# A short convolution, a truncated Fourier mix and a product with its ReLU: x fetched two rows to a partition, the convolution worked by row parities in four quadrants of the array

## The chip, the cores and the metric

One core of one Trainium2 chip runs the whole kernel. The metric is the time of one execution in device microseconds (us); less is better. The kernel before was timed three times: median 177.82 us (177.51 to 178.9). A separate execution was profiled; its own time was 176.57 us.

## The reference

`x` has 8 sequences of 3264 rows and 192 columns (float32). `weight` has 7 taps for each of 8 heads; a head is 24 neighbouring columns. Three steps follow each other:

```python
# 1. causal convolution along the rows, one softmaxed 7-tap filter per head
w = softmax(weight, axis=-1)
c[b, s, h, :] = sum(w[h, k] * x_padded[b, s + k, h, :] for k in range(7))   # 6 zero rows in front
# 2. the 64 lowest Fourier modes of c along the rows, each multiplied by its own 192 x 192 complex matrix
C = rfft(c, axis=1)[:, :64]
Y = C @ (w_r + 1j * w_i)              # one matrix for each mode; the other modes are zero
u = c + irfft(Y, n=3264)
# 3. a product, a ReLU and a sum
out = u + maximum(u @ w_ch, 0)
```

The 64 complex matrices are 18.9 MB, `x` is 20.05 MB and `out` is 20.05 MB. The kernel fetches x and the matrices with a conversion to bfloat16 on the way.

## The kernel before

**Order.** The instructions of each engine stand in the order in which the program was written; the schedule is by hand, and the engines wait for each other by semaphores. All fetches of x and of the matrices are issued by POOL, in order; SP issues the stores. There are three stages.

**The convolution stage** works on four pairs of sequences (`q` is 0 to 3, two sequences `i` to each). A pair's rows are cut into 128-row tiles, one row to a partition, and `load_unit` (L141) fetches some tiles at a time: 13 double tiles (`b`) for each pair, in four units for the first pair and three for the others (`units`). A row of a tile is 192 values, so one DMA packet writes 384 bytes. The convolution along the rows is a matrix product with a banded matrix (`band`): row r of the output is a weighted sum of rows r-6 to r. The band is built at the start: seven masks (L178), seven predicated copies (L193) into `packed`, and four copies (L199, L201) that shift it for groups of 32 partitions. `conv_pass` (L269) does two heads of a unit: a main product with the tile itself and a corner product with the tile before it. Two instructions run side by side, each with 64 columns of the array (`tile_position` (0, 0) and (0, 64)); between them they give the even rows (`a` = 0) and the odd rows (`a` = 1) of a double tile as separate output tiles, which is the order that the later stages want. Results lie in three accumulators of two PSUM banks each (`ZC`), and ScalarE (L290) and VectorE (L292) take turns to copy them back over x in SBUF.

**The Fourier products** (`dft`, L295) are put between the passes: one output tile of c against a table of cosines and sines (`ftab`), 26 tiles to a pair, each as two instructions of 64 columns side by side. The table itself is computed by `table` (L206) on VectorE and ScalarE in three parts during the first pair; the dictionary `extra` says after which pass. When a pair is done, `xtrans` (L307) turns its result round.

**The mix stage** begins when all four pairs are done. `mix(g, bank)` (L421) multiplies with the matrices of four modes; g runs from 0 to 15. `load_w(g)` (L261) fetches the matrices in two DMAs; eight groups have places at once, and group 8 and later ones are fetched when an earlier `mix` has given its place free. Between the mixes `some` runs the transposes of c (L387) that the last stage needs.

**The output stage** (L642 and around it) forms u @ w_ch and the inverse transform in one accumulator for each tile, 64 rows of the array at a time; ScalarE applies the ReLU (L558), VectorE adds c (L545) and SP stores. There `turn` (L483) already exists: an empty instruction on TensorE that waits until named matmuls have ended, so that the lower and the upper half of the array do not write one PSUM bank at the same time.

## The time and the profile before

| what | value |
|---|---|
| median of three runs | 177.82 us (177.51 to 178.9) |
| the profiled execution's own time | 176.57 us |
| its span, first to last instruction | 174.6 us |
| TensorE matmul busy | 160.1 us (92%), 2756 instructions |
| VectorE, ScalarE, POOL busy | 122.0, 106.9, 58.6 us |
| granted TensorE clock | 0.995 of full speed |
| moved by DMA | 40.11 MB |
| convolution matmuls (L283) | 832 instructions, 39.1 us busy |
| Fourier products (L301) | 208 instructions, 20.9 us busy |
| copies back by VectorE (L292), by ScalarE (L290) | 26 for 24.8 us, 26 for 20.6 us |

Times in the profile count from the first instruction; the profiled execution took 1.97 us more than the span. A row of the list of groups gives the source line, the engine, the operation, what it writes and reads with its shape, how often it ran, then the busy time in us and the mean of one in ns, and after the bar the idle time of the engine just before. PE is TensorE's matmul, PEld its loading of the stationary operand, DVE VectorE, ACT ScalarE. The end of a matmul is modelled: the mean of one contains its way through the array, so the pace is read from starts, not from durations.

### The profile page before, as it was taken

What the parts mean: (1) busy time and instruction counts of PE and PEld (TensorE: products, weight loads), DVE (VectorE), ACT (ScalarE), POOL (GpSimd) and SP (SyncE); (2) the same over time, 40 slices, a digit from 0 to 9 for tenths busy, and PEclk for the clock granted to TensorE, in tenths of its full rate; (3) what the DMA queues carried; (4) which work ended last, traced back from release to release, by engine and by line L of the source; (5) the groups of instructions that cost most, each with busy time, mean ns of one, the idle gap of its engine ahead of it and who ended that gap; (6) DMA issues with size and microseconds to landing.
All of it is one profiled execution on the core that took longest, in us unless ns stands there. A gap on an engine that the chain in (4) does not pass through costs nothing.

```text
span 174.6 us, 6593 instructions
## 1 busy us (share of the span) xinstructions
PE 160.1 (92%) x2756; PEld 139.7 (80%) x2756; DVE 122.0 (70%) x226; ACT 106.9 (61%) x191; POOL 58.6 (34%) x101
## 2 busy tenths in 40 slices
PE   7967999999999988999967978999999999999990
PEld 2447989999998966899966545599999999999960
DVE  5669883274454562777745225699999999999991
ACT  6337885434544342787645244588788888887870
POOL 7999943465322344424344000592000000000000
PEclk9999999999999999999999999999999999999998
DMA  4999999999999999999999980289989899999896
GB/s 46 168 188 192 191 194 192 191 192 193 193 193 194 203 206 207 205 207 206 206 207 206 207 147 9 70 301 327 367 305 341 334 332 360 341 343 333 324 345 226
DMA packets 50541, 40.11 MB, mean 230 GB/s; under 512 B 28720, under 2 KB 50512, under 8 KB 50512
## 3 DMA queue, kind: packets, MB, share of 16 engines
q0 software_dynamic: 36000, 19.62, 81.2%
q1 hardware_dynamic: 14512, 20.09, 31.5%
q8 instruction: 21, 0.34, 0.8%
q14 instruction: 8, 0.07, 0.1%
HBM read 39.10 MB, written 20.05 MB: 339 GB/s over the span
## 4 chain that ended last, share of the span: by engine, by line
PE 72%; DMA 13%; DVE 5%; ACT 4%; issue 2%; POOL 1%; DVEq 0%; POOLq 0%; ACTq 0%
PE z L642 33%; PE z L283 19%; DMA arena<-in_moe_w_i_dram 13%; PE z L301 10%; PE z L387 4%; DVE arena L193 2%; PE z L426 2%; ACT xall L290 1%; DVE xall L292 1%; PE z L569 1%; POOL xall L148 1%; PE z L512 1%; ACT L184 1%; DVE arena L545 1%; PE z L316 1%
## 5 line engine op out<-in xcount | busy, mean ns | idle before, releaser
L545 DVE TENSOR_TENSOR arena<-z,xall 128x384 f32<-128x384 f32 (+1 forms) x104 | 57.5, 557 | 3.1 <-PE z L642 1.1
L558 ACT ACTIVATE z<-z 128x384 f32<-128x384 f32 x102 | 48.3, 475 | 12.6 <-PE z L642 3.6
L642 PE MATMUL z<-arena,ftab 64*128 64x384 bf16 x308 | 45.3, 323 | 0.0
L642 PEld LDWEIGHTS <-ct 64*128 64x128 bf16 x600 | 42.4, 94 | 1.9 <-PE z L569 0.6
L642 PE MATMUL z<-wsw,ct 64*128 64x192 bf16 x300 | 42.2, 243 | 0.0
L283 PE MATMUL z<-xall,shared 128*64 128x192 bf16 (+3 forms) x832 | 39.1, 246 | 2.6 <-ACT shared L199 1.5
L283 PEld LDWEIGHTS <-shared 128*64 128x64 bf16 x832 | 36.3, 110 | 5.0 <-ACT shared L199 2.0
L292 DVE CAST xall<-z 128x768 bf16<-128x768 f32 (+3 forms) x26 | 24.8, 956 | 21.9 <-PE z L283 18.9
L642 PE MATMUL z<-wm,ct 64*128 64x192 bf16 x200 | 34.1, 243 | 0.0
L290 ACT CAST xall<-z 128x768 bf16<-128x768 f32 (+3 forms) x26 | 20.6, 795 | 19.4 <-PE z L283 19.3
L642 PEld LDWEIGHTS <-ftab 64*128 64x128 bf16 x396 | 26.6, 93 | 1.4 <-issue 0.8
L148 POOL DMA_DIRECT2D xall<-in_x_dram x26 | 23.7, 920 | 11.3 <-DMA xall<-in_x_dram 10.4
L642 PE MATMUL z<-w,ct 64*128 64x192 bf16 x100 | 24.3, 243 | 0.0
L379 DVE COPY ct<-z 128x1024 bf16<-128x1024 bf16 x26 | 17.1, 687 | 8.0 <-PE z L387 4.8
L301 PE MATMUL z<-xall,ftab 128*64 128x384 bf16 (+1 forms) x208 | 20.9, 326 | 0.7 <-ACT xall L290 0.7
L387 PE MATMUL z<-ident,xall 128*128 128x128 bf16 x312 | 19.3, 220 | 0.2 <-ACT ftab L377 0.2
L387 PEld LDWEIGHTS <-xall 128*128 128x128 bf16 x312 | 17.7, 98 | 0.9 <-issue 0.3
L377 ACT COPY ct<-z 128x1024 bf16<-128x1024 bf16 x13 | 13.2, 1012 | 4.2 <-PE z L387 4.0
L301 PEld LDWEIGHTS <-ftab 128*64 128x64 bf16 (+1 forms) x208 | 13.1, 110 | 2.6 <-DVE xall L292 0.6
L642 PE MATMUL z<-mixa,ftab 64*128 64x384 bf16 x88 | 13.8, 323 | 0.0
L453 POOL DMA_DIRECT2D arena<-ylate x16 | 7.9, 504 | 15.8 <-ACT ylate L449 15.8
L264 POOL DMA_DIRECT2D arena<-in_moe_w_r_dram x13 | 8.0, 613 | 14.9 <-PE z L387 5.7
(108 smaller groups left out, 133.4 us busy)
## 6 DMA issues: line engine op xcount, KB each, us to landing
out_dram<-arena SPq DMA_DIRECT2D x47, 384.0 KB, 3.4
xall<-in_x_dram POOLq DMA_DIRECT2D x14, 384.0 KB, 13.1
arena<-in_moe_w_r_dram POOLq DMA_DIRECT2D x13, 288.0 KB, 11.4
arena<-in_moe_w_i_dram POOLq DMA_DIRECT2D x13, 288.0 KB, 11.7
xall<-in_x_dram POOLq DMA_DIRECT2D x6, 432.0 KB, 13.6
ct<-in_moe_w_r_dram POOLq DMA_DIRECT2D x3, 288.0 KB, 11.8
ct<-in_moe_w_i_dram POOLq DMA_DIRECT2D x3, 288.0 KB, 11.3
out_dram<-arena SPq DMA_DIRECT2D x3, 288.0 KB, 3.6
```

The source lines that it names most:

```text
L148: nc.gpsimd.dma_start(out=xall[:, s0:s0 + nf, i, :], in_=src)
L264: nc.gpsimd.dma_start(out=wts[g][64 * half:64 * half + 64, :, :, :], in_=src[4 * g:4 * g + 4, :, :].rearrange("m (p j) e -> p m j e", j=3))
L283: nc.tensor.matmul(o, lhs, xall[:, r0:r0 + 2 * n - 1:2, :, dsl], start=(main and a == 0), stop=not main, tile_position=(0, 64 * half), ski ...
L290: nc.scalar.copy(out=dst, in_=srcv)
L292: nc.vector.tensor_copy(out=dst, in_=srcv)
L301: nc.tensor.matmul(xp[r, :], ftab[0:k, t, r], xall[0:k, NT * q + t, :, :], start=(t == 0), stop=(t == NT - 1), tile_position=(0, 64 * hh), ...
L377: nc.scalar.copy(out=out, in_=in_)
L379: nc.vector.tensor_copy(out=out, in_=in_)
L387: nc.tensor.matmul(o, in_, ident[:], start=True, stop=True, is_transpose=True)
L545: nc.vector.tensor_tensor(out=o[0:pn, :, a, :], in0=bank[0:pn, 0:2 * D].rearrange("p (i d) -> p i d", i=2), in1=xall[0:pn, s + a, :, :], o ...
L558: nc.scalar.activation(out=z, in_=z, func=ACT.Relu)
L642: mm = nc.tensor.matmul(target(bank[k], cols, r), l, r, start=first, stop=last, skip_group_check=True)
```

## The change

x is fetched two neighbouring rows to a partition: a block is 256 rows, a packet writes 768 bytes, and there are fewer and larger units (three for the first pair: 3, 5 and 5 blocks; two for the others: 7 and 6). A partition's first row is the even one and its second the odd one, so the convolution goes by parities: output rows of parity `a` are a sum over input rows of parity `a1`. The band becomes one for equal and one for unequal parities (`band[..., o, ...]`), with four masks, fourteen smaller predicated copies and eight shifting copies, done for four heads first and then for the other four.

The array is used in four quadrants of 64 rows and 64 columns. `conv_pieces` gives, for one unit, one head and one output parity, four instructions for the lower rows (`row` = 0) and four for the upper rows (`row` = 1); the corner product with the block before it falls to one of the quadrants. `conv_step` writes the lower pieces of the present step and the upper pieces of the step two before it in turns, after a `turn` that waits for that older step's lower pieces. Each step has one PSUM bank out of seven; after every second step VectorE copies back the even result and ScalarE the odd one. A Fourier product becomes one instruction over all 128 columns. The numbers of Fourier products between steps, the places of the table's parts, and the number of warming matmuls at the start (28, not 30) change with it. The mix stage and the output stage keep their code.

```diff
-    NSLOT = NQ * NT + 1
-    PW = 32 + KK - 1
+    NSLOT = NQ * NT + 2
+    PW = 32 + KK // 2
+    BW = P + 2
-    NIDLE = 30
-    UNITS0 = ((0, 2), (2, 3), (5, 4), (9, 4))
-    UNITS = ((0, 4), (4, 4), (8, 5))
+    NIDLE = 28
+    UNITS0 = ((0, 3), (3, 5), (8, 5))
+    UNITS = ((0, 7), (7, 6))
...
+    xin = xall[:, :, :, :].rearrange("p (b x) i d -> p b (x i d)", x=2)
+    xin5 = xin.rearrange("p b (i a d) -> p b i a d", i=2, a=2)
...
-    ZC = [zl[0], zl[1], zr[2]]
-    zf = zr[0:2]
+    ZC = [z[:, 0, :] for z in zl + zr[0:3]]
+    zf = zr[3][:, 0, 0:2 * D]
 
     def load_unit(q, b0, n):
...
-            src = bass.AP(tensor=x.tensor, offset=x.offset + off, ap=[[D, P], [P * D, nf], [1, D]])
-            nc.gpsimd.dma_start(out=xall[:, s0:s0 + nf, i, :], in_=src)
+            src = bass.AP(tensor=x.tensor, offset=x.offset + off, ap=[[2 * D, P], [2 * P * D, nf], [1, 2 * D]])
+            nc.gpsimd.dma_start(out=xin[:, s0:s0 + nf, 2 * D * i:2 * D * (i + 1)], in_=src)
...
-    for k in range(KK):
-        nc.vector.copy_predicated(out=pk3,
-                                  mask=masks[:, PW * k:PW * (k + 1)].unsqueeze(1).to_broadcast([P, H, PW]),
-                                  data=ta3[:, :, k:k + 1].to_broadcast([P, H, PW]))
...
+    for h0 in (0, H // 2):
+        hs = slice(h0, h0 + H // 2)
+        for lag in range(KK):
+            k = lag // 2
+            nc.vector.copy_predicated(
+                out=pk4[:, hs, lag % 2, :],
+                mask=masks[:, PW * k:PW * (k + 1)].unsqueeze(1).to_broadcast([P, H // 2, PW]),
+                data=ta3[:, hs, KK - 1 - lag:KK - lag].to_broadcast([P, H // 2, PW]))
...
-    def conv_pass(q, b0, n, h2):
...
+    def conv_pieces(step, row):
+
+        (q, b0, n, h, a), z = step
+        s0 = NB * q + b0 + 1
+        r = slice(64 * row, 64 * row + 64)
+        dsl = slice(GRP * h, GRP * h + GRP)
+        for a1 in range(2):
+            for col in (row, 1 - row):
+                c0 = (0 if a < a1 else 1) + (64 if col != row else 0)
+                s1 = s0 - 1 if (row, col) == (1, 0) else s0
+                o = z[64 * col:64 * col + 64, 0:2 * GRP * n].rearrange("p (b i e) -> p b i e", b=n, i=2)
+                yield nc.tensor.matmul(o, band[r, h, int(a != a1), c0:c0 + 64], xin5[r, s1:s1 + n, :, a1, dsl],
+                                       start=(row == 0 and a1 == 0), stop=(row == 1 and a1 == 1),
+                                       tile_position=(64 * row, 64 * col), skip_group_check=True).ins.name
...
+    def conv_step(u):
...
+        if u is not None:
+            flow[-1] = [(u, conv_bank()), []]
+            lower = conv_pieces(flow[-1][0], 0)
+        old = flow[-3] if len(flow) > 2 else None
+        if old is not None:
+            turn(old[1][2:])
+            upper = conv_pieces(old[0], 1)
+        for _ in range(4):
+            if u is not None:
+                flow[-1][1].append(next(lower))
+            next(upper, None)
+        if old is not None and old[0][0][4] == 1:
+            for (q, b0, n, h, a), z in (flow[-4][0], old[0]):
...
+                if a == 0:
+                    nc.vector.tensor_copy(out=dst, in_=srcv)
+                else:
+                    nc.scalar.copy(out=dst, in_=srcv)
 
     def dft(q, t0, t1):
-        xp = zf[q % 2][:, 0, 0:2 * D]
+        xp = zf
...
-            for hh in range(2):
-                r = slice(64 * hh, 64 * hh + 64)
-                nc.tensor.matmul(xp[r, :], ftab[0:k, t, r], xall[0:k, NT * q + t, :, :],
-                                 start=(t == 0), stop=(t == NT - 1), tile_position=(0, 64 * hh),
-                                 skip_group_check=True)
+            nc.tensor.matmul(xp, ftab[0:k, t, :], xall[0:k, NT * q + t, :, :],
+                             start=(t == 0), stop=(t == NT - 1), skip_group_check=True)
...
+            if k == 1 and h in (5, 7):
+                dfts(3)
+            elif k > 1 and h in (3, 7):
+                dfts(5 if k < 4 else 7)
-        if k == 4:
+        if k == 3:
             for g in range(NW + 3):
                 load_w(g)
         todo.append((u[0], 2 * u[1], 2 * (u[1] + u[2])))
+    for _ in range(2):
+        conv_step(None)
     dfts(99)
```

## The prediction

> **What bounds the kernel now.** I read the page's busy times and chain first, then windows cut at the stages' borders, then single instructions.
>
> ```profile
> PE 160.1 (92%) x2756; PEld 139.7 (80%) x2756; DVE 122.0 (70%) x226; ACT 106.9 (61%) x191; POOL 58.6 (34%) x101
> ...
> PE 72%; DMA 13%; DVE 5%; ACT 4%; issue 2%; POOL 1%; DVEq 0%; POOLq 0%; ACTq 0%
> ```
>
> TensorE holds most of the chain, a transfer 13%. Where each of them binds is shown by the windows: the first pair's convolution, the rest of that stage, the mix stage, then four slices of 5 us (PE, PEld, DVE, ACT, POOL busy; clock; DMA share; GB/s as written).
>
> ```profile
> 11.57:23.69 12.12, 11.01 (x278) 10.35 (x278) 10.06 (x16) 9.47 (x14) 10.67 (x20) 1.00 1.60 192
> 23.69:67.10 43.41, 42.68 (x802) 39.37 (x802) 22.09 (x25) 19.98 (x28) 17.79 (x24) 1.00 1.51 195
> 67.10:106.09 38.99, 34.48 (x624) 28.70 (x627) 21.78 (x41) 22.18 (x37) 11.91 (x20) 1.00 1.13 193
> ...
> 5.00:10.00 5.00, 5.00 (x22) 2.05 (x20) 3.72 (x10) 1.45 (x2) 4.86 (x10) 1.00 1.51 172
> 20.00:25.00 5.00, 4.81 (x108) 4.57 (x104) 4.37 (x6) 3.79 (x7) 3.43 (x5) 1.00 1.60 192
> 55.00:60.00 5.00, 5.00 (x108) 4.43 (x104) 3.30 (x4) 2.29 (x5) 1.45 (x3) 1.00 1.41 201
> 75.00:80.00 5.00, 5.00 (x104) 4.77 (x102) 4.11 (x8) 3.71 (x6) 1.93 (x4) 1.00 1.21 207
> ```
>
> From 23.69 to 67.10 TensorE is busy 42.68 of 43.41 us. DMA is full too: x until the share falls near 58 us (1.60 to 1.21), then matrices at 207 GB/s. TensorE's pace, from the chain in time (start, length, instructions):
>
> ```profile
> 26.18 1.32 PE z L283 x32
> 27.49 0.97 PE z L301 x12
> ```
>
> 32 convolution matmuls of 192 columns in 1.32 us are 16 pairs of 82.5 ns; 6 pairs of 384 columns take 162 each. That is columns/2.4 + 2.5 ns, weights hidden. Next, where the mix stage waits (timeline):
>
> ```profile
> 82.74 0.25 PE L426 MATMUL z<-ct,mixa 128*16 128x192 bf16 x3
> 82.92 0.29 PE L387 MATMUL z<-ident,xall 128*128 128x128 bf16 x2
> ...
> 88.76 0.46 PE L426 MATMUL z<-arena,mixa 128*16 128x192 bf16 x12 [1.49 <-DMA arena<-in_moe_w_i_dram]
> 94.49 0.46 PE L426 MATMUL z<-arena,mixa 128*16 128x192 bf16 x12 [0.97 <-DMA arena<-in_moe_w_i_dram]
> ...
> 96.73 0.24 PE L503 MATMUL z<-w,ct 64*128 64x192 bf16 x1
> 97.04 0.25 PE L503 MATMUL z<-wm,ct 64*128 64x192 bf16 x1
> ...
> 103.05 0.46 PE L426 MATMUL z<-arena,mixa 128*16 128x192 bf16 x12 [0.22 <-DMA arena<-in_moe_w_i_dram]
> ```
>
> TensorE waits for matrices 1.49 + 0.97 + 0.22, and 0.15 more when the starts around 103.05 and around the mix at 100.22 are held against the pace: **2.83 us** in all, the stage's whole slack. Between these waits it runs from 68.92, where the first mix starts, without a pause that a transfer ends. The chain's 13% DMA is a row of transfers of 11 to 12 us behind each other; take them away and TensorE is next, 2.83 us earlier. So a convolution stage that ends x us later moves the end by x - 2.83, down to -2.83 at x = 0.
>
> **The change part by part.**
>
> *Fetch of x.* 16 engines at 192 GB/s spend 32.0 ns on a packet of 384 bytes, at 207 GB/s 89.0 ns on one of 1152; the line between gives 60.5 ns for 768, or 203 GB/s. By 10 us 1.16 MB are in (60 and 172 GB/s); the other 8.87 of x's 10.03 MB take 43.7 us, so x is in at 53.7 instead of about 58. Unit 3 (the second pair's first) completes 3.88 MB: 23.4 and landing, 23.8. At the old rate it would be 24.6. The fetches go from 28 to 22; the second pair's now stands behind POOL's `ident` and `perm`, but 2.51 MB are queued ahead of it, enough until 17 us. The matrices' fetches follow about 4 us earlier; group 8 needs the first mix, long before the eight groups ahead of it are in.
>
> The Trainium skill (DMA: Bandwidth & Descriptors, Specifications) asks for at least 512 bytes for line rate. The 384-byte packets lose only 7% here; if by that rule 768 bytes ran at the full 207, unit 3 would land 0.3 us sooner, which is inside the bounds below.
>
> *Start.* Four masks for seven save 3 x 0.103 = 0.31 us (L178: seven took 0.72). A predicated copy of 304 elements takes 478 ns (L193); small VectorE operations of 56 elements take 220, so 140 elements are 280 on that line (ends: 220 in proportion, 478 unchanged), 310 with the hand-over. Seven for four heads: 6.67 to 8.85; ScalarE's two shifting copies of 442 ns end at 9.75. The convolution starts near 9.8 instead of 11.57, the warming matmuls being done at 9.6. But VectorE then builds the other four heads, to 12.1, before it can copy any result.
>
> *Copies back.* These are the rows for the price:
>
> ```profile
> L292 DVE CAST xall<-z 128x768 bf16<-128x768 f32 x16 | 15.3, 957 | 13.5 <-PE z L283 11.1 <-ACT xall L290 1.7 <-ACT mixa L327 0.6
> L292 DVE CAST xall<-z 128x384 bf16<-128x384 f32 x2 | 1.1, 556 | 1.2 <-PE z L283 1.2
> ```
>
> (957 - 556)/384 = 1.04 ns an element and 155 ns fixed: 506, 456, 406 and 305 ns for units of 7, 6, 5 and 3 blocks. 26 become 72.
>
> *First pair.* VectorE: 8 x 305 + 16 x 406 + tables 6.04 (L210, L213, L215 at 0.54, 0.36, 0.54 for 6 tiles and twice 0.82, 0.66, 0.82 for 10) = 15.0 us, less the last three copies (1.2), which TensorE need not await. Neighbours overlap: before, the durations of what began from 12.49 to 22.68 add up to 11.3 us and were 10.06 busy, so 13.8 become 12.3, from 12.1 to 24.4 without a pause; with the 17% idle of before, 26.9. TensorE's own work would be done by 23, unit 3 lands at 23.8. I take **25.0** for the start of unit 3 (ends 23.8 and 26.9), nearest to the uninterrupted row, since seven single banks give more room than three double ones.
>
> *The other three pairs.* A step is two rounds of four quadrants. In L283 two column halves run at full pace together, in L426 four column strips, in the output stage two row halves: I take four quadrants at once, at columns/2.4 + 2.5. A step of 7 blocks (336 columns) is 285 ns, of 6 (288) 245. Ends: that, or two abreast, twice as long.
> - Convolution: 3 x 16 x (285 + 245) = 25.4; last upper halves 0.5; last copy 0.76.
> - Fourier products: 88 x 162.5 = 14.3, as before, only whole instead of halves.
> - Turning: 3 x 0.34 = 1.0.
> - New: the quadrants have another tile shape than the 128-column products and the 64-column turning; before, all three had one shape. 82.74 to 82.92 is a change of shape: 178 ns where 82.5 is the pace, so 95 ns lost. 12 stretches of products are entered and left, 3 turnings too, and the last entry: 31 x 95 = 2.9. No row shows quadrants; ends 0 and twice that. No other work hides it.
> - 0.45 of other losses, as before (43.41 against 42.96 by the same list).
>
> Sum 45.4, so the products end at 25.0 + 45.4 = 70.4, not 67.1: 3.3 late. The copies of this part are on other engines: VectorE needs 506 of the 570 ns of two steps.
>
> *The added wait.* `turn` is an instruction of TensorE's own queue, so every later matmul, lower pieces of the new step included, stands behind it, and behind those both copying engines. 96.73 to 97.04 is such a wait right behind its matmul: 307 ns, of which 80 streaming. A step may start 2 x columns/2.4 + 230 ns after the step two before it: 510 against the natural 570 (7 blocks), 470 against 490 (6): free, barely. With 5 and 3 blocks 430 against 410 and 350 against 250: a few us at most, under VectorE's time for the first pair.
>
> **Sum.** +3.3 - 2.83 = +0.5 us on the profiled execution's 176.57 (span 174.6 and 1.97 around it): 177.1. The median of the runs is 177.82, so I predict **178.3**.
>
> **Rivals.**
> - *Faster.* The first pair goes as fast as its data: unit 3 at 23.8, and shape changes cost half (-1.5): +0.6 - 2.83 = -2.2, or 175.6. The early start speaks for it; 15.0 us of VectorE work against it.
> - *Slower: the copies set the pace.* A bank is taken again seven steps later; of these, four pass until its pair's last upper piece has started, and 166 ns of array (a matmul of 192 columns lasts 246, 80 of them streaming), the copy and two hand-overs must fit into the other three. With 40 ns each (as seen at the first copies) the step must be at least (166 + 80 + 456)/3 = 234 ns at 6 blocks, 251 at 7: free. It decides once hand-over and queueing pass 110 ns at 6 blocks. With 300 in all the steps become 307 and 324: 48 x 62 + 48 x 39 = 4.8 us, or 183.1. For it: VectorE at 89%, with nothing to spare at 6 blocks. The Trainium skill (TensorEngine Tiling (Array Packing), PSUM Bottleneck) says that after tiling the copy out of PSUM may become the limit; by the rows here it just doesn't.
> - *Slower: `turn`.* 100 ns more in each steady wait: 48 x 40 + 48 x 20 = 2.9 us, or 181.2.
> - *It doesn't do what it says:* two quadrants at a time. +25 us, about 203.
> - x no faster for its packets: unit 3 at 24.6, under the 25.0; no difference.
>
> **Chances.** Forecast (within 1%, 1.8 us, about what a measurement of this kernel can tell from no change) 0.42; faster 0.24; copies 0.18; `turn` 0.12; two abreast 0.04. So 0.24 / 0.42 / 0.34. The likeliest case alone runs from 176.5 to 179.9. The range reaches down to -2.83 (175.0) and up to the copies' 183.1; two abreast and worse bank stalls are left out.
>
> **What would show it.** Right: the last Fourier product ends near 70 and the first mix starts near 72; the convolution starts near 9.8; steps of 285 and 245 ns; 95 ns lost at each shape change; mixes without waits for matrices, which land about 4 us earlier. Wrong: VectorE copies idle and the first pair over by 23; TensorE waiting for L292 in every step; `turn` visible as idle time ahead of the convolution; a mix that still waits for a transfer.

## The result, and the profile after

The changed kernel takes 184.32 us (median of 4 runs, 183.77 to 184.88) against 177.67 us (177.51 to 178.90) of the kernel before beside it: **3.6% slower** (ratio 1.0359, 95% interval 1.0302 to 1.0416). The prediction was 178.3 us with a range from 175.0 to 183.1. The profiled execution took 184.13 us, its span 182.3 (before 176.57 and 174.6).

The page of the changed kernel: busy times, the granted clock and the transfer rate in 40 slices of 4.56 us, the chain.

```profile
PE 167.5 (92%) x2970; PEld 123.9 (68%) x2970; DVE 129.2 (71%) x278; ACT 113.8 (62%) x239; POOL 52.2 (29%) x95
...
PEclk9996999999999999999999999999999999999999
...
GB/s 48 149 198 203 207 201 203 205 206 199 204 204 207 206 207 206 201 51 160 198 207 94 162 191 39 0 168 305 351 323 347 319 363 316 366 332 341 351 343 229
...
PE 83%; DVE 9%; ACT 3%; issue 2%; DVEq 0%; ACTq 0%
```

Transfers have left the chain (13% before, nothing now): no mix waits for a matrix any more, and x comes at 198 to 207 GB/s (203 on average from 10 us to its end). VectorE has gone from 5% to 9% of the chain. The 6 in the fourth place of the clock's row is new: before, all were 9 but the last. The same three stages as in the prediction, as windows of the changed kernel (columns: length; PE, PEld, DVE, ACT, POOL busy; clock; DMA share; GB/s):

```profile
9.90:28.91 19.01, 16.14 (x394) 10.55 (x394) 15.22 (x43) 13.49 (x34) 10.72 (x20) 0.91 1.31 203
28.91:77.96 49.05, 47.18 (x904) 27.40 (x904) 25.29 (x53) 23.67 (x57) 15.14 (x24) 1.00 1.26 204
77.96:114.03 36.07, 33.73 (x621) 28.51 (x618) 21.96 (x42) 22.11 (x37) 9.83 (x16) 1.00 0.85 137
```

| | before | after | difference |
|---|---|---|---|
| convolution starts | 11.57 | 9.90 | -1.67 |
| first pair | 12.12 | 19.01 | +6.89 |
| other three pairs, to the end of the products | 43.39 | 49.05 | +5.66 |
| from there to the start of the last mix | 38.96 | 36.07 | -2.89 |
| rest | 68.52 | 68.30 | -0.22 |

So the first pair and the other pairs lose about as much each, and the mix stage gives back what it waited for matrices before.

Three places show where the time goes. First, the first pair. The timelines of VectorE and of TensorE in the changed kernel (start, length, what; in brackets the idle time before it and what ended it):

```profile
10.74 1.02 DVE L205 COPY_PREDICATED arena<-arena 128x140 bf16<-128x140 uint16 x4
11.79 0.46 DVE L215 COPY shared<-arena 32x280 bf16<-32x280 bf16 x2
12.38 0.56 DVE L326 CAST xall<-z 128x144 bf16<-128x144 f32 x1
```

```profile
10.74 0.71 PE L299 MATMUL z<-xall,shared 64*64 64x144 bf16 x24
13.01 0.44 PE L299 MATMUL z<-xall,shared 64*64 64x144 bf16 x16 [1.56 <-DVE xall L326]
```

The early start runs seven steps into seven banks, until 11.45; then TensorE stands still for 1.56 us until VectorE has built the band's second half and made its first copy (12.38 to 12.94). And what follows runs at half the clock (windows of 1 us, the clock third from the right):

```profile
14.00:15.00 1.00, 0.86 (x32) 0.65 (x28) 1.00 (x5) 0.47 (x2) 1.00 (x2) 0.79 1.32 204
15.00:16.00 1.00, 0.95 (x30) 0.80 (x31) 0.56 (x3) 1.00 (x4) 1.00 (x2) 0.50 1.31 202
16.00:17.00 1.00, 1.00 (x30) 0.78 (x25) 0.90 (x2) 0.96 (x4) 0.89 (x2) 0.50 1.34 213
17.00:18.00 1.00, 1.00 (x28) 0.83 (x24) 0.91 (x3) 0.48 (x2) 0.27 (x1) 0.50 1.28 194
18.00:19.00 1.00, 1.00 (x35) 0.65 (x27) 0.77 (x3) 0.61 (x3) 0.00 (x0) 1.00 1.32 203
```

That is 0.42 + 3 us at 0.50; steps of 5 blocks take 400 to 434 ns there and 230 to 235 later. For the pair as a whole, these are the windows from VectorE's first copy to the second pair, the changed kernel and then the kernel before:

```profile
12.38:28.91 16.53, 14.59 (x346) 9.43 (x345) 12.85 (x33) 12.61 (x32) 8.38 (x13) 0.90 1.32 204
12.49:23.69 11.20, 10.10 (x245) 9.43 (x238) 10.06 (x16) 9.13 (x14) 9.75 (x19) 1.00 1.60 192
```

VectorE is busy for 2.79 us more, and it stands idle for 3.68 us where it was 1.14 before. Second, the turning in the other pairs (TensorE's timeline, changed kernel):

```profile
37.83 0.95 PE L299 MATMUL z<-xall,shared 64*64 64x288 bf16 x24
39.10 0.44 PE L299 MATMUL z<-xall,shared 64*64 64x288 bf16 x8 [0.33 <-DVE xall L326]
```

The third step behind each turning takes 760 ns instead of 245: the turning has taken two of the seven banks, and TensorE stands still until a copy by VectorE has ended. Third, ahead of the first mix (waits of the changed kernel from 77 to 81 us):

```profile
DVE z L402 <- ACT xs L337: 2.4, 1, 2.4
```

The memset of a mix bank stands in VectorE's queue until ScalarE has copied the one Fourier bank that is left, since it is the same bank. The first mix starts 2.24 us behind the products' end, 1.85 before.

### The profile page after: what moved, and what is told of

It is laid out like the page before. It is cut to its first block, busy times and chain, and to the rows that moved or that the text cites. A ratio compares the mean times of both kernels' runs of the same rounds, so it can differ in the third digit from the quotient of the medians.

```text
span 182.3 us, 7178 instructions
## 1 busy us (share of the span) xinstructions
PE 167.5 (92%) x2970; PEld 123.9 (68%) x2970; DVE 129.2 (71%) x278; ACT 113.8 (62%) x239; POOL 52.2 (29%) x95
## 4 chain that ended last, share of the span: by engine, by line
PE 83%; DVE 9%; ACT 3%; issue 2%; DVEq 0%; ACTq 0%
PE z L667 32%; PE z L299 21%; PE z L419 11%; PE z L334 10%; PE z L458 3%; DVE xall L326 2%; DVE arena L205 2%; PE z L537 1%; PE z L346 1%; PE z L594 1%; PE z L605 1%; PE z L528 1%; DVE xall L175 1%; PE z L538 1%; ACT L191 1%
## 5 line engine op out<-in xcount | busy, mean ns | idle before, releaser
L583 ACT ACTIVATE z<-z 128x384 f32<-128x384 f32 x102 | 48.5, 475 | 12.1 <-PE z L667 2.4
L326 DVE CAST xall<-z 128x336 bf16<-128x336 f32 (+3 forms) x72 | 32.0, 448 | 25.5 <-PE z L299 22.3
L299 PE MATMUL z<-xall,shared 64*64 64x288 bf16 (+3 forms) x1152 | 44.1, 290 | 4.9 <-DVE xall L326 3.8
L328 ACT CAST xall<-z 128x336 bf16<-128x336 f32 (+3 forms) x72 | 27.6, 388 | 24.5 <-PE z L299 21.3
L299 PEld LDWEIGHTS <-shared 64*64 64x64 bf16 x1152 | 27.4, 108 | 21.5 <-issue 9.4
L667 PE MATMUL z<-wsw,ct 64*128 64x192 bf16 x300 | 35.1, 243 | 0.0
L667 PE MATMUL z<-wm,ct 64*128 64x192 bf16 x200 | 29.9, 243 | 0.0
L334 PE MATMUL z<-xall,ftab 128*128 128x384 bf16 (+1 forms) x104 | 19.8, 327 | 0.6 <-DVE xall L326 0.6
L150 POOL DMA_DIRECT2D xall<-in_x_dram x18 | 15.8, 879 | 12.3 <-DMA xall<-in_x_dram 11.4
L334 PEld LDWEIGHTS <-ftab 128*128 128x128 bf16 (+1 forms) x104 | 8.9, 98 | 9.0 <-issue 4.5
L485 POOL DMA_DIRECT2D arena<-xs x16 | 7.9, 504 | 14.7 <-ACT xs L481 14.6
## 6 DMA issues: line engine op xcount, KB each, us to landing
ct<-in_moe_w_r_dram POOLq DMA_DIRECT2D x3, 288.0 KB, 11.7
ct<-in_moe_w_i_dram POOLq DMA_DIRECT2D x3, 288.0 KB, 11.7
```

Of the source, the lines that this page charges most:

```text
L150: nc.gpsimd.dma_start(out=xin[:, s0:s0 + nf, 2 * D * i:2 * D * (i + 1)], in_=src)
L299: yield nc.tensor.matmul(o, band[r, h, int(a != a1), c0:c0 + 64], xin5[r, s1:s1 + n, :, a1, dsl], start=(row == 0 and a1 == 0), stop=(row ...
L326: nc.vector.tensor_copy(out=dst, in_=srcv)
L328: nc.scalar.copy(out=dst, in_=srcv)
L334: nc.tensor.matmul(xp, ftab[0:k, t, :], xall[0:k, NT * q + t, :, :], start=(t == 0), stop=(t == NT - 1), skip_group_check=True)
L583: nc.scalar.activation(out=z, in_=z, func=ACT.Relu)
```

## The experiments

Times in us: *second pair* is the start of its first convolution matmul, *last product* that of the last Fourier product. In the kernel after the change they are 28.91 and 77.64, the time 184.13. Each of e1 to e9, e11, e13 and e14 was executed once. Four executions of the changed kernel took 183.77 to 184.88, and the start of the convolution, which e1, e2, e3, e5, e9, e13 and e14 leave as it is, lies anywhere from 9.89 to 10.55 in them: a difference of some tenths of a microsecond in the time or in one place shows nothing by itself; the stretch between two places of one trace says more.

**One wait at a time.** e1 issues all four lower pieces of a step ahead of the wait for the bank's turn:

```
-            turn(old[1][2:])
             upper = conv_pieces(old[0], 1)
         for _ in range(4):
             if u is not None:
                 flow[-1][1].append(next(lower))
+        if old is not None:
+            turn(old[1][2:])
+        for _ in range(4):
             next(upper, None)
```

e2 exchanges the engines of the copies back (`if a == 0` becomes `if a == 1`: even results on ScalarE, odd ones on VectorE). e3 moves the turning behind the unit's first stretch of products (from `h == 1` to `h == 3`). e4 leaves the second and third part of the Fourier table out and sets them to zero on POOL (`nc.gpsimd.memset(ftab[:, 6:NT, :], 0.0)`), so that 20 of 26 tiles are multiplied with zeros.

> All four lower pieces of a step are written ahead of the wait, and only the upper pieces behind it; the work is the same. In the changed kernel a step of 6 blocks has a natural pace of 245 ns, but eight of them from 55.90 to 58.12 take 2.22 us, steps of 243 to 324. Theory A: the wait for the lower pieces sets this pace, since the new lower pieces stand behind it; then the steps of 6 blocks fall to 245 to 250 and the last Fourier product ends 1 to 1.5 us sooner than 77.96 us. Theory B: the return of the banks from the copying engines sets it; then nothing changes, within 0.3 us.

> ScalarE copies the even results and VectorE the odd ones, the reverse of the changed kernel. The bank of the even result is the older one and is due 3 steps after its copy may start; ScalarE needs 398 ns for 6 blocks where VectorE needs 457. Theory B (banks): 60 ns are won at every place where TensorE waits for the even result's copy, some 20 places after the first pair, so the last Fourier product ends 1 us sooner than 77.96. Theory A (the wait among the matmuls): no change there. Both expect little in the first pair, where both copying engines are full.

> The turning of a pair's result moves from the middle of the convolution steps (after the second head) to just behind the unit's first stretch of Fourier products. In the changed kernel it takes two of the seven banks while the convolution runs, and the third step after it waits until 69.47 for VectorE, 0.49 us late. Theory: these waits go, and one change of shape with each, so the last Fourier product ends 3 x 0.6 = 1.8 us sooner than 77.96. Rival: the wait comes from VectorE's own extra copy and only moves; then at most 0.3 us.

> The second and third part of the table of cosines and sines are left out (tiles 6 to 25 hold zeros, written once by POOL): six operations of VectorE, 4.6 us, and six of ScalarE, 5.3 us, in the first pair. Everything else stays. Theory: the first pair, 9.90 to 28.91 us, is late because TensorE, VectorE and ScalarE wait for each other in turn and the copying engines have the most to do; then the second pair starts at 25.7 to 26.5, when its data have landed (25.73), and the end comes some 2.5 to 3 us sooner. Rival: the start of the second pair is set by data or by the band's second half; then it moves by less than 1 us.

| | second pair | last product | between them | time |
|---|---|---|---|---|
| after | 28.91 | 77.64 | 48.73 | 184.13 |
| e1, lower pieces first | 28.47 | 77.46 | 48.98 | 184.06 |
| e2, engines exchanged | 29.87 | 77.42 | 47.56 | 184.16 |
| e3, turning moved | 28.68 | 77.22 | 48.54 | 184.06 |
| e4, table parts out | 31.78 | 80.73 | 48.95 | 187.46 |

e1: in a unit of 6 blocks four of the sixteen steps fell to 245 to 248 ns (from 270, 285, 261 and 262), so the turn's wait was real, but the bank waits behind it grew (323 to 353, 760 to 776 ns), and from the second pair to the last product nothing was won. e2: the bank waits shrink (323 to 260, 760 to 698 ns) and the three pairs gain 1.17, as theory B has it (0.23 of it in a step of unit 3, 501 ns instead of 734, which is no bank's; see the last section); the second pair starts 0.96 later, 0.41 of it because the convolution does, the rest in the first pair, where ScalarE also builds tables. e3: the wait behind the turning only moves with it (steps of 759 ns again). Each wait that goes is taken over by the next one.

e4 came out the wrong way round. POOL's zeros and VectorE's copies that shift the band run at the same time (timelines of POOL and VectorE in e4):

```profile
10.69 2.26 POOL L247 MEMSET ftab<- 128x2560 bf16 x1
```

```profile
9.40 4.08 DVE L215 COPY shared<-arena 32x280 bf16<-32x280 bf16 x2
```

The two copies took 4.08 instead of 0.65, and the convolution started at 13.27. So e4 can't say what the tables cost. From VectorE's first copy (16.01) to the second pair it still took 15.77 us against 16.53, though VectorE was busy for 9.86 instead of 12.85; but 6.84 us ran at a clock of 0.50, twice as long as in the changed kernel, so this doesn't weigh the two against each other either.

**The gap and the clock.** e5 fills the time in which TensorE waits with matmuls whose results nothing reads; e6 builds the band at once for all heads (`for h0 in (0,): hs = slice(0, H)`), with 38 idle matmuls ahead; e9 is e5 with the tables cut finer.

```
                 conv_step((*u, h, a))
+                if (k, h, a) == (0, 3, 0):
+                    for _ in range(18):
+                        nc.tensor.matmul(zr[3][:, 0, 0:2 * BW], band[:, 0, 0, 0:P], bandrow[:, 0:2 * BW], ...)
```

> Behind the seventh convolution step of unit 0, 18 matmuls of 260 columns of the band's first head are run into the Fourier bank (nothing reads their results; 18 x 110 ns = 2.0 us), so that TensorE isn't idle while VectorE builds the band's second half. Theory A, the clock: in the kernel after the change TensorE is idle from 11.5 to 13.5 us and its granted clock is then 0.5 in the stretches 15:16 to 17:18, where steps of 5 blocks take 400 to 434 ns instead of 235. With the gap filled the clock stays 1.00, unit 1's steps fall below 290 ns, the second pair's convolution starts at 27.2 to 27.9 (28.91 in the kernel after the change), the last product at 75.9 to 76.6 (77.64), and the time is 182.4 to 183.1 (184.13). Theory B, VectorE's queue sets the first pair and the clock only lies beside it: the clock is 1.00, but the steps stay long by waits for VectorE's copies, the second pair starts at 28.6 to 29.2 and the time is within 0.3 us of 184.13.

> The band is built once for all heads (7 predicated copies and 4 shifting copies over 8 heads instead of twice over 4), and the idle matmuls ahead are 38 instead of 28, to cover the later start. Theory A: the wait for VectorE at the seventh bank (1.88 us) and the halved clock behind it (1.4 us) come from the second half of the band, which stands in VectorE's queue ahead of the first copy back. Then the convolution starts at 11.4 to 12.2 (9.90), has no wait over 0.8 us in unit 0, the clock is 1.00 to 26 us, the second pair starts at 26.5 to 27.5 (28.91) and the time is 181.7 to 182.7. Theory B: VectorE has the same work before unit 3 whichever way it is cut, so the second pair stays at 28.5 to 29.3 and the time within 0.4 us of 184.13.

> The filled gap of e5 (182.97 us; second pair from 28.29, last product 76.59), and in addition the two table parts of 10 tiles are cut into four of 5 and one step of a part stands behind each head, up to the fifth head of unit 3; the tables' work is the same but for some fixed costs. Theory: what is left in the first pair is that a table step of 640 columns (0.81 us) stands in VectorE's queue between two copies back, longer than the ring of seven banks lasts. Then steps of 500 us and more disappear from units 1 and 2 (in e5: 615, 826, 735 ns), the second pair starts at 26.0 to 27.2, the last product at 74.4 to 75.6, and the time is 180.8 to 182. Rival: VectorE's total in the first pair counts, however it is cut; then the second pair starts at 27.9 to 28.6 and the time is 182.6 to 183.3.

| | convolution | second pair | last product | time |
|---|---|---|---|---|
| e5, gap filled | 9.91 | 28.29 | 76.59 | 182.97 |
| e6, band at once | 11.36 | 28.94 | 77.57 | 184.21 |
| e9, gap filled, tables cut finer | 10.13 | 28.29 | 76.71 | 183.71 |

In e5 the clock stays full (a window of e5, as above):

```profile
14.00:15.00 1.00, 0.77 (x32) 0.62 (x29) 1.00 (x5) 0.64 (x3) 1.00 (x2) 1.00 1.35 215
```

The second pair starts 0.61 sooner, between the two theories (27.2 to 27.9, 28.6 to 29.2): with a full clock TensorE waits for VectorE instead (0.77 busy). The last product comes 1.05 sooner, in theory A's range, but the other 0.43 arise behind the first pair, where one step of unit 3 takes 315 ns instead of 734 (see the last section). So the low clock costs the first pair 0.6, or up to 1.1, as the filling matmuls last 0.47 longer than the gap. e6 has neither the gap nor the low clock and isn't faster at all: its first pair takes 17.58 instead of 19.01, and it starts 1.47 later. e9: cutting the table steps gains nothing (the expectation's "500 us" is meant as 500 ns); the rival is right on the second pair (27.9 to 28.6), though the time came 0.4 above its range.

**The fetch.** e7 splits each fetch of x into even and odd rows, so that packets have 384 bytes as before, while everything lands in the same place:

```
-            ... ap=[[2 * D, P], [2 * P * D, nf], [1, 2 * D]])
+            for a in range(2):
+                ... offset=x.offset + off + a * D, ap=[[2 * D, P], [2 * P * D, nf], [1, D]])
```

> x goes to the same places, but each fetch is split into one for the even rows and one for the odd rows, so that a packet has 384 B as in the kernel before, not 768. If packet length is what made x faster (206 against 192 GB/s at the pages' slices), x arrives at 192 to 195 GB/s and is all there at 59.5 to 60.8 (56.79). If the fetch isn't on the path that sets the end, the second pair starts at 28.6 to 29.3 and the time is within 0.3 us of 184.13; if it is, every unit lands up to 1.5 us later (unit 3 at 27.2 against 25.73) and the time is 184.8 to 186.

x came at 192 GB/s and was in at 59.86 (56.79 after the change); second pair 29.12, last product 77.99, time 184.68. The second pair is where it was expected if the fetch doesn't hold the end (28.6 to 29.3); the time is 0.55 later, more than the 0.3 expected, but the last product is 0.35 later, less than the 0.47 by which the convolution starts later (10.37), and that start varies as much without the edit. The longer packets (in 22 fetches instead of 40) bring x 3 us sooner, and no gain of the kernel by it can be seen.

**TensorE's code, a theory that fell.** TensorE starts again late at about its 961st instruction in the changed kernel, and at about its 449th, 705th or 961st in several experiments (matmuls, weight loads and the sequencer's waits in the profile), multiples of 256 apart, in part with a copy still running, 1.2 to 1.5 us behind the last packet of a 16 KB fetch on the instruction queue. e11 gives the first pair two units, which is 256 instructions fewer (it also cuts the tables in four parts and does 8 Fourier products ahead of the second pair, not 16); e13 and e14 add to e5 the same time of TensorE in 72 and in 18 instructions.

```
-    UNITS0 = ((0, 3), (3, 5), (8, 5))
-    UNITS = ((0, 7), (7, 6))
+    UNITS0 = UNITS = ((0, 7), (7, 6))
```

> The kernel after the change with the first pair in two units of 7 and 6 blocks like the others, not three of 3, 5 and 5: 256 instructions of TensorE fewer (128 matmuls with their weight loads), 8 first products at the end of unit 1 and 18 in unit 2, the tables in four parts. Theory C, TensorE's own code: in the kernel after the change a block of 256 instructions (16 KB on the instruction queue) is fetched every 6.1 us in the first 47 us, each block's first instruction runs 1.3 to 1.5 us behind its last packet, and instructions 449, 705 and 961 of TensorE stand at 19.09, 25.06 and 31.35 us; in e6, e8 and e10 TensorE stands still 0.5 to 1.5 us just ahead of 449 and 705 with no semaphore outstanding. By it a later start (unit 0 has 7 blocks, which land at about 13) costs less than the 256 instructions save: convolution from 12.8 to 13.8 (9.90), instruction 449 at 20.8 to 22, the second pair at 25.4 to 26.8 (28.91), the last product at 74.2 to 75.6 (77.64), time 180.8 to 182.2 (184.13). Theory B, VectorE's queue: its tables and copies from 12.3 on sum to 14 us, the second pair then starts at 27 to 28.9 and the time is 182.5 to 184.2.

> The kernel of e5 (gap filled; second pair 28.29, 182.97 us), and behind each of nine heads, from head 4 of unit 0 to head 4 of unit 1, four more matmuls of 128 columns into the Fourier bank, which nothing reads: 72 instructions of TensorE, some 9 x 0.23 = 2.1 us of its time. Theory C (the fetching of TensorE's code, 256 instructions per 6.05 us, holds the first pair from about 17.7 us on): the second pair starts 72 x 23.6 ns = 1.7 us later than in e5, at 29.7 to 30.3, 1.0 to 1.5 us later than in e14. Theory B (VectorE holds it; TensorE's steps of unit 1 wait for it in any case): no difference from e14 (within 0.3 us), and within 1 us of e5.

> The same as e13 with one matmul of 512 columns behind each of the nine heads instead of four of 128: as much time of TensorE (9 x 0.216 = 1.9 us), but 18 instructions instead of 72. Theory C: second pair 18 x 23.6 ns = 0.4 us later than in e5, at 28.5 to 29.0, and 1.0 to 1.5 us earlier than e13. Theory B: the same as e13 within 0.3 us.

| | convolution | second pair | last product | time |
|---|---|---|---|---|
| e11, two units | 11.61 | 25.59 | 75.85 | 182.58 |
| e13, 72 instructions | 10.55 | 30.69 | 78.99 | 185.45 |
| e14, 18 instructions | 9.89 | 29.99 | 78.28 | 185.01 |

e11's second pair is where theory C had it (the last product 0.25 later than expected; the time, 182.58, is in theory B's range), 3.3 sooner than after the change though the convolution starts 1.7 later and the clock is at 0.50 from 11.7 to 15.1. 1.3 of the 3.3 are the eight products that come later (8 x 0.1625); at the last product 1.8 are left. But e13 and e14 differ by 0.70, of which 0.65 is the convolution's start: the number of instructions doesn't matter there. Theory C is out for the first pair, and theory B is half right: e13 equals e14, but neither is within 1 us of e5. What they do show is that 1.9 to 2.1 us more of TensorE's time (the expectations' estimate) delay the second pair by 1.7, convolution starts apart: TensorE's waits in the first pair aren't room beside VectorE's work. The reading that fits these runs is that the two take turns, TensorE waiting for a bank and VectorE for a step, so that time put on TensorE comes on top. Whether time put on VectorE does so too, and how much of the turn ScalarE holds (busy 12.61 of 16.53), wasn't tried by itself. e11, with fewer and larger steps, gains the most of the runs so far.

**All together.** These runs take several waits away at once:

> Several edits at once: the band built once with 38 idle matmuls ahead, the lower pieces of a step ahead of the wait for the bank's turn, from the second pair on the even results copied back by ScalarE and the odd ones by VectorE, one stretch of products to a unit instead of two, and the Fourier bank exchanged so that the memset ahead of the mixes doesn't wait for its copy. If the losses are separate: 2.0 us in the first pair, 1.2 by the engines of the copies, 8 stretches less at two shape changes of 95 ns each 1.5, the memset 0.4, the turn 0.2, together 5.3: the last product starts at 72.4 to 73.6 (77.64) and the time is 178.7 to 180. If the losses replace one another, as with the single edits so far (each within 0.1 us of 184.13 at the end): last product 75 to 77, time 181.5 to 183.5.

> The edits of e8 (182.55 us; second pair 29.98, from there to the last product 46.09), with 34 idle matmuls, the tables spread as in e9, the turning placed in the Fourier bank and one bank of the ring instead of two of the ring, and the last unit's stretch of products cut 9 to 5 around the last two convolution steps. If each takes away its own wait: second pair at 26.0 to 27.2 (-3.3), turning's waits (three of 0.47 us) halved -0.7, wait of the last products behind the last copy (0.77 us) -0.6: the last product starts at 71 to 72.5 and the time is 177.0 to 178.6, that of the kernel before (178.71 in the run on this chip, median 177.67) within 1%. If VectorE's total sets the first pair, 179.5 to 181, slower than before by 1% or more.

> The edits of e10 (180.65 us, second pair 29.18, from there to the last product 45.35) with the first pair in two units as in e11, 44 idle matmuls, and the last unit's products cut 9 to 5 as there. By theory C the second pair starts at 25.4 to 26.8 and the last product at 70.6 to 72.4, if the other pairs keep their 45.35: time 176.6 to 178.5, within 1% of the kernel before (177.6). If the other pairs are held by the code too (e10: instructions 705 to 2239 in six blocks of 6.08 us), they cannot become shorter, and lengthen if fewer instructions are fetched ahead; the time is then 178 to 179.5. By theory B the second pair starts at 27.5 or later and the time is 179 to 180.7.

> e12 (178.73 us; convolution from 13.88 behind 44 idle matmuls, x of unit 0 there at 11.48) with 34 idle matmuls instead of 44, so that the convolution starts at 11.5 to 12.6. Theory C: the first block's end is reached sooner by as much, the second pair starts at 24.6 to 25.5 (26.32), where its x, there at 24.6, holds it, and the time is 177.0 to 178.0, the kernel before (177.69) within 0.5% on either side. Theory B: VectorE has 12.8 us of copies and table steps from its first copy on before the second pair, so the start moves it little: second pair 25.6 to 26.4, time 178.0 to 178.8.

> e15 (177.72 us; TensorE idle from 23.5 to 25.2 until x of unit 2 is there at 25.07; steps of unit 2 up to 625 ns behind table steps) with the other pairs in units of 6 and 7 blocks instead of 7 and 6, so that unit 2's x is there one block (about 1 us) sooner, with the last table part's three VectorE steps placed ahead of unit 2, where VectorE is idle, 11 products instead of 8 ahead of unit 2, and the last unit's products cut 7 to 5. If x is what holds the first pair now and VectorE's tables hold unit 2: unit 2 from 24.0 to 24.6 (25.20), 1.0 to 1.7 us less to the last product (71.68), time 176.0 to 176.8, against 176.84 of the kernel before: 0.0 to 0.5% faster. If the first pair is held by the turns of TensorE and VectorE in any order, unit 2 starts at 24.8 to 25.5 and the time stays at 177.3 to 177.9, slower than before by 0.3 to 0.6%.

> e16 (177.51 us, 0.9978 of the kernel before; unit 2 takes 5.55 us against 4.13 of the same unit of the later pairs, with ScalarE busy by table steps of 0.53 to 0.75 us between its copies, while VectorE waits 1.6 us there) with VectorE copying the even results of heads 1 and 3 of unit 2 in place of ScalarE. If ScalarE's queue holds unit 2, two copies of 0.39 us less on it shorten unit 2 by 0.4 to 0.8 us: last product at 70.3 to 70.7 (71.06), time 0.4 to 0.8 us under that of e16 beside the same kernel before, 0.993 to 0.996 of it. If the two engines' turns with TensorE hold it, it stays within 0.2 us.

The less obvious edits, from e8 (one stretch, banks), e10 (turning, last unit) and e17 (ScalarE relieved):

```
-            if k == 1 and h in (5, 7):
-                dfts(3)
-            elif k > 1 and h in (3, 7):
-                dfts(5 if k < 4 else 7)
+            if k > 0 and h == 7:
+                dfts(99)
...
-    ZC = [z[:, 0, :] for z in zl + zr[0:3]]
-    zf = zr[3][:, 0, 0:2 * D]
+    ZC = [z[:, 0, :] for z in zl + zr[1:4]]
+    zf = zr[0][:, 0, 0:2 * D]
...
-            banks = [conv_bank(), conv_bank()]
+            banks = [zr[0][:, 0, :], conv_bank()]
...
-                if a == 0:
+                if (a == 0) == (q == 0) or (q, b0) == (1, 0) and h in (1, 3):
                     nc.vector.tensor_copy(out=dst, in_=srcv)
```

| | second pair | last product | time (median) | against before, 95% interval |
|---|---|---|---|---|
| e8 | 29.98 | 76.08 | 182.55 | - |
| e10 | 29.18 | 74.53 | 180.65 | 1.0183 (1.0138 to 1.0228) |
| e12 | 26.32 | 72.84 | 178.73 | 1.0053 (1.0017 to 1.0090) |
| e15 | 25.20 | 71.68 | 177.72 | 1.0039 (1.0023 to 1.0054) |
| e16 | 24.47 | 71.06 | 177.51 | 0.9978 (0.9952 to 1.0005) |
| e17 | 24.19 | 70.32 | 176.93 | 1.0001 (0.9986 to 1.0017) |

e8 won less than the sum of its parts (1.6 of 5.3): its convolution started at 12.28, and its second pair 1.1 later than after the change instead of 2.0 sooner. e10's second pair (29.18) isn't where it was expected either (26.0 to 27.2); e12's, with two units, is (25.4 to 26.8). e12 and e15 do 8 Fourier products ahead of the second pair, e16 and e17 do 11, e8 and e10 16 as after the change, the kernel before 10; the last product has no such difference. In e15 x holds the first pair at last, as theory C's text had it for another reason: unit 2's x is there at 25.07, and TensorE and VectorE stand idle for it (a window of e15):

```profile
24.00:25.00 1.00, 0.00 (x0) 0.00 (x0) 0.00 (x0) 0.00 (x0) 0.00 (x0) 1.00 1.33 207
```

e16's smaller unit there starts the second pair where expected, but only 0.62 of the 1.0 to 1.7 arrive at the last product (the ratio, 0.9978, is in the range that was expected, 0 to 0.5% faster, and its interval holds 1); e17's two copies less on ScalarE's queue shorten unit 2 from 5.55 to 5.09 and bring the last product to 70.32, as expected, but not the time against the kernel before (1.0001, where 0.993 to 0.996 was expected). There it ends: **e17 is as fast as the kernel before, and none of these is measurably faster.** The stages of e17, as windows, say why:

```profile
11.58:24.19 12.61, 11.88 (x260) 8.99 (x259) 11.18 (x27) 9.85 (x23) 7.27 (x17) 1.00 1.31 204
24.19:70.64 46.45, 46.16 (x909) 33.92 (x909) 27.01 (x59) 24.97 (x59) 15.60 (x25) 1.00 1.28 204
70.64:106.20 35.56, 33.72 (x620) 28.50 (x617) 21.61 (x41) 22.14 (x37) 9.83 (x16) 1.00 1.04 175
```

The first pair takes as long as before (12.61 against 12.12). The other pairs take 3.06 longer than before. The quadrant steps themselves aren't the price: 48 of 285 and 48 of 245 ns and the last upper halves (0.5) are 25.9 us, as much as the convolution's instructions took before from start to start. By the paces above, 19 changes of shape at 93 ns are 1.8; unit 2 takes 0.95 more than the same unit of a later pair, the other waits between steps are some 1.3, and the products take 1.2 less than before. The mix stage is 3.40 shorter, as it no longer waits for matrices.

## Why the prediction was wrong

Its frame held: the stages, the mechanism of the slack, and most prices. **Two terms of the sum failed, both about waiting for the copies back.**

- *First pair, "I take 25.0 for the start of unit 3" (23.8 to 26.9): 28.91.* This is the larger error, +3.9. The step that failed is the overlap: VectorE's work "from 12.1 to 24.4 without a pause", with TensorE's work and the data beside it. The work was sized right: from its first copy at 12.38 on VectorE is busy for 12.85 us (12.3 predicted). What was put at next to nothing is its idle time, 3.68 us: in 2.0 of it VectorE waits for TensorE's steps, while TensorE waits 2.8 us for VectorE's copies; e13 and e14 show that TensorE's waits aren't spare time. The sentence "seven single banks give more room than three double ones" is what was wrong: seven steps of 3 blocks last about 1.5 us, less than VectorE's pause for the second half of the band, 9.90 to 12.38, which I had named in the working of the start and then left out of TensorE's row. The clock was on no list; it cost 0.6 to 1.1 (e5). The gap and the clock aren't most of the error, though: in e6, which has neither, the first pair still takes 17.58 us where 15.2 were predicted (9.8 to 25.0). That rest is spread over many steps; that it is the two engines' turns is the reading of e13 and e14, and no run takes it apart further.
- *Other three pairs, 45.4: 49.05, +3.7.* The turning was priced at its own matmuls, 3 x 0.34; that it holds two banks of seven was left out, and this is 0.5 each time, 1.5 in all (0.18 each time in e17, where it takes one bank of the ring). Another 0.45 is the late start at unit 3's eighth step (734 ns for 285), which no copy explains (see the last section). The remaining 1.7 come in pieces of less than 0.1: bank waits of 23 to 78 ns, `turn` at 6 blocks, called free, "barely", with 14 to 40 ns in four steps of sixteen, and the stretches of products, each of which costs some 70 ns beyond its two changes of shape (232 ns in the step that holds it and 25 in the next, for 2 x 93). e1 shows that without the wait of `turn` the banks take the same time. The mechanism of the rival "the copies set the pace" is what came, as single long waits rather than as a longer step; e2, with the engines exchanged, supports it.
- *Missing: +0.4 ahead of the first mix.* The change leaves one Fourier bank and it is also a mix bank, so the memset waits. The diff shows it, and in e8, with the banks exchanged, the first mix starts 1.75 us behind the products' end (2.24 after the change, 1.85 before).
- *Slack 2.83:* the first mix is 11.28 later and the last 7.99: 3.29 given back. The form "end moves by x - 2.83" holds within 0.5 when x is taken at the first mix, in e17 too (3.46 later, 3.30 given back).
- *Right:* steps of 7 blocks at 285 ns, so four quadrants run at once; a change of shape costs 92 to 94 ns (235 ns from the last quadrant matmul to the product, of which 142.5 are its own; 256 from the last product to the next quadrant, 162.5 its own; predicted 95); copies back at 507, 458, 404 ns (506, 456, 406) for 7, 6 and 5 blocks, though the 128x144 copies took 330 for 305 (the largest and the smallest, from the groups of the changed kernel):

```profile
L326 DVE CAST xall<-z 128x336 bf16<-128x336 f32 x24 | 12.2, 507 | 9.3 <-PE z L299 8.0
L326 DVE CAST xall<-z 128x144 bf16<-128x144 f32 x8 | 2.6, 330 | 0.5 <-ACT xall L328 0.4
```

- *Right by luck:* the convolution starts at 9.90 (9.8). The predicated copies began at 7.60, not 6.67, and took 251 ns each with the hand-over, not 310 (the line through the working's two rows gives 307 for 140 elements, not its 280); and the first steps started when one of ScalarE's two shifting copies had ended, where the working waits for both. These errors cancel.
- *The fetch:* the rate was right (203), but unit 3 landed at 25.73 instead of 23.8 and x at 56.79 instead of 53.7. The first 10 us moved 1.07 MB, not 1.16, which is 0.5 us; the rest is that other transfers came between: from 10 to 56.79 us 9.5 MB moved, where x needed 9.0. In the changed kernel nothing waited for x, so this cost nothing; in e15 x did hold the second pair.

With most of the waits removed the change costs next to nothing: +0.2 us in e17's span (174.8 against 174.6), where +0.5 was predicted. That the two agree is in part luck, not a proof of the sum. e17 starts the convolution at 11.58, not 9.8, and the second pair at 24.19, not 25.0; its other pairs take 46.45, not 45.4, although it enters and leaves only about half as many stretches of products. What e17 shows is that the changed kernel's loss was waits which can be removed; the sum left them out.

## What to carry to other kernels

Where two engines hand banks to each other, add up what each needs in a window of as many steps as there are banks, not over the stage: a pause of the copying engine longer than that window stops the other, even if both have idle time in the stage as a whole. Count every user of the ring, the rare ones too, which take banks out of it for several steps. And when single edits each take a wait away and the end doesn't move, take all of them away in one kernel before deciding what the change itself is worth.

## What was not expected

- *The clock.* TensorE idle for 1.1 to 2.2 us early in the kernel was followed by a clock of 0.50 for about 3.4 us (3.42 by the windows of the changed kernel) in six kernels, the changed one, e1, e2, e3, e7 and e11, and for 6.84, twice that, in e4 (2.85 us idle). 1.52 us idle in the kernel before, from 10.05 to 11.57, was followed by none, nor were 1.16 in e8, 1.28 in e10 and 1.43 in e15. The Trainium skill (TensorE: Matmul & The Clock Gate, Part 1) tells of a free-running window of about 3.4 us by which the clock is set, and has the clock fall after a whole idle window. The 3.42 agree with the first; on the second the runs differ, as less than half of such a window was enough in the changed kernel, e2, e3 and e7. That the window runs freely would explain why the length of the gap alone doesn't decide; no run here shows it.
- *POOL beside VectorE.* A memset of 2.26 us on POOL was accompanied by two VectorE copies of 32 partitions that took 4.08 us together instead of 0.65 (e4); the first ended at 13.17, 0.23 behind the memset. Its mechanism wasn't tried.
- *Code.* The instruction queue brought 23 blocks of 16 KB, one each 6.1 us while x came. At about the 961st instruction of the changed kernel, unit 3's eighth step, TensorE goes on at 31.35, 0.47 us behind the end of the last copy it could wait for and 1.45 behind the block's last packet. The step ahead of it (734 ns there) takes 501, 880, 602 and 879 in e2, e3, e4 and e7, where TensorE goes on 1.2 to 1.4 us behind that block's last packet, and 315 to 317 in e5, e13 and e14, which have more instructions ahead of it, so that the block's border falls on another step. The Trainium skill (Runtime: NRT & Kernel Launch, Instruction fetch mechanics) has blocks of 256 instructions and says that their fetching is hidden. Here some tenths of a microsecond may not have been: these runs speak for it, but none was made to try it. e13 and e14 show that it isn't what bounds the first pair, and the rest stays open.
